# SwiGLU feed-forward on one core: the first loads in line on SyncE, and slice 0 projected ahead of the second transposes

## The chip, the cores and the metric

One Trainium2 chip, one of its cores. A core has a matrix engine (TensorE, "PE"), a vector engine (VectorE, "DVE"), a scalar engine (ScalarE, "ACT"), GpSimd ("POOL") and SyncE ("SP"), each with an instruction queue of its own, and 16 DMA engines that move data between the off-chip memory and the on-chip memory. The metric is the device time of one execution in microseconds (us). The kernel before takes 163.57 us, the median of three runs (163.53 to 163.64).

## The reference

All tensors are bfloat16. The kernel computes a SwiGLU feed-forward block for 2048 rows of 640 columns, with an inner width of 1536:

```python
B, S, D, F = 1, 2048, 640, 1536      # x: [B, S, D]; w_gate, w_up: [D, F]; w_down: [F, D]

def reference(x, w_gate, w_up, w_down):
    g = _silu(x @ w_gate)
    u = x @ w_up
    return (g * u) @ w_down
```

## The kernel before

The rows are worked in four blocks of 512. The gate and up projections are computed transposed: a chunk of 128 inner columns of a weight is the stationary operand, x transposed (`xT`, 128 model columns on the partitions, five such slices of 128) is the moving one, and five matmuls, one for each slice of the model dimension, add up in one bank of PSUM. ScalarE applies Silu to the gate result, VectorE multiplies it with the up result and writes `aT`. When the twelve inner chunks of a block are done, the down projection follows from `aT` and `w_down`. VectorE has a side task: it computes the last four rows of the projections as dot products.

What the change touches is the start, block 0.

Loads. x rows 0-255 are loaded as they lie, in two pieces of 128 rows (line 86, 160 KB each): the first is issued from SyncE, the second from ScalarE. The gate weights of the first four inner chunks (`EARLY`) are loaded as five slices, one for each 128 rows of `w_gate` (line 115, 128 KB each): slice 1 from ScalarE, the others from SyncE. Behind them SyncE issues, in this order, the load that transposes rows 256-511 on the way (`turn_x`, line 105), the up weights of chunks 0-1 and 2-3 (line 83, 320 KB each), the remaining gate and up weights (640 KB each), `w_down` (line 125), and the next block's transposing load. Each DMA has one of eight semaphores in turn; an issue waits until the earlier DMA with its semaphore has landed.

TensorE, in the order in which `head` writes it down (an order that is kept by dependencies without a wait): 18 warm-up matmuls on a tile of ones that nothing reads (line 176); five transposes of x rows 0-127 and five of rows 128-255 (line 185), each group of five in two PSUM tiles, of which ScalarE copies the first (slices 0 and 1) and VectorE the second (slices 2 to 4) to `xT` (line 190); then the gate projection of four chunks at once, in steps of four matmuls (line 193):

```python
steps = [(0, 0, P), (0, P, HALF)]
steps += [(kd, 0, HALF) for kd in range(1, KD)]
steps += [(kd, HALF, S_BLK) for kd in range(KD)]
```

A step is (slice, first column, end column): slice 0 on rows 0-127, on rows 128-255, the slices 1 to 4 on rows 0-255, and all five on rows 256-511, which come by the transposing load. After that the up projection of the four chunks and their gating (lines 214 and 215), and from there the plain loops.

ScalarE issues its two DMAs, loads its table for Silu and runs a dummy Silu (line 119), and then takes its copies.

Of the kernel before, what the change touches and what calls it, by code (L numbers as in the profile page):

```python
# [10 lines left out]
def _body(  # L11
# [8 lines left out]
    nc = tc.nc  # L20
    P = nc.NUM_PARTITIONS
    f32 = mybir.dt.float32
    bf16 = mybir.dt.bfloat16
    ACT = mybir.ActivationFunctionType
# [8 lines left out]
    KD = D // P  # L33
    KF = F // P
    S_BLK = 512
    NSB = S // S_BLK
    SUB = S_BLK // P
    HALF = S_BLK // 2
    DA = 512
    Q = 32  # L40
    N_WARM = 18
    T = 4
    WT_STEP = 4
    ROW_J = 0
    EARLY = 4
# [13 lines left out]
    wg_sb = consts.tile([P, KD, F], bf16)  # L59
# [15 lines left out]
    wg_v = w_gate.rearrange("(kd p) f -> p kd f", p=P)  # L75
# [3 lines left out]
    def wslice(a, b):  # L79
        return slice(a * P, b * P)  # L80
# [4 lines left out]
    def load_x(eng, c0, c1):  # L85
        eng.dma_start(out=x_sb[:, c0:c1, :], in_=x_v[:, c0:c1, :])  # L86
# [11 lines left out]
    def keep_order(engine):  # L98

        traced = [i for i in nc.cur_bb.bb.instructions if i.engine == engine]  # L100
        for a, b in zip(traced, traced[1:]):
            issue_order(a, b)

    def turn_x(r0, r1):
        nc.sync.dma_start_transpose(out=xT[:, :, r0:r1], in_=xt_v[r0:r1])

    ones = consts.tile([P, P], bf16)
    silu_first = consts.tile([P, 1], f32)
    nc.vector.memset(ones[:], 1.0)  # L109

    load_x(nc.sync, 0, 1)
    load_x(nc.scalar, 1, 2)
    for kd in range(KD):
        eng = nc.scalar if kd == 1 else nc.sync
        eng.dma_start(
            out=wg_sb[:, kd, wslice(0, EARLY)], in_=wg_v[:, kd, wslice(0, EARLY)]
        )
    turn_x(HALF, S_BLK)
    nc.scalar.activation(silu_first[:], ones[:, 0:1], ACT.Silu)  # L119
    for a in range(0, EARLY, 2):  # L120
        load_w(nc.sync, wu_sb, wu_v, a, a + 2)
    for a, b in W_CHUNKS:
# [6 lines left out]
    def turn_w(dst, src, f0, f1):  # L129
# [7 lines left out]
        out=x_row[:],  # L137
        in_=x2[S - T : S, :].rearrange("t d -> (t d)").partition_broadcast(P),
# [35 lines left out]
    def warm(n):  # L174
        for _ in range(n):
            nc.tensor.matmul(  # L176
                pw[:, 0:P], lhsT=ones[:], rhs=ones[:], start=True, stop=True
            )

    def transpose_chunk(c, parts):  # L180
        c_sl = slice(c * P, (c + 1) * P)
        for copy, tag, k0, k1 in parts:
            pt = psum.tile([P, k1 - k0, P], bf16, tag=tag, name="pt")
            for kd in range(k0, k1):
                nc.tensor.transpose(  # L185
                    out=pt[:, kd - k0, :],
                    in_=x_sb[:, c, kd * P : (kd + 1) * P],
                    identity=ident[:],
                )
            copy(out=xT[:, k0:k1, c_sl], in_=pt[:])  # L190

    def proj_step(ps, w_sb, fc, sb, c0, c1, kd):
        nc.tensor.matmul(  # L193
            ps[:, c0:c1],
            lhsT=w_sb[:, kd, fc * P : (fc + 1) * P],
            rhs=xT[:, kd, sb * S_BLK + c0 : sb * S_BLK + c1],
            start=(kd == 0 and c0 in (0, HALF)),
            stop=(kd == KD - 1),
        )

    def proj(ps, w_sb, fc, sb, c0, c1):
        for kd in range(KD):
            proj_step(ps, w_sb, fc, sb, c0, c1, kd)
# [6 lines left out]
    def gate(pg, pu, sb, fc, n_s):  # L210

        s0 = sb * S_BLK
        sg = work.tile([P, S_BLK], f32, name="sg")
        nc.scalar.activation(sg[:, 0:n_s], pg[:, 0:n_s], ACT.Silu)  # L214
        nc.vector.tensor_tensor(  # L215
            out=aT[:, fc, s0 : s0 + n_s], in0=sg[:, 0:n_s], in1=pu[:, 0:n_s], op=ALU.mult
        )

    def head():
        dve, act = nc.vector.tensor_copy, nc.scalar.copy  # L220
        split = [(act, "po_a", 0, 2), (dve, "po_b", 2, KD)]
        pgs = [
            psum.tile([P, S_BLK], f32, tag="gu", name="pg", bufs=4)
            for _ in range(EARLY)
        ]
        warm(N_WARM)
        for c in range(HALF // P):
            transpose_chunk(c, split)

        steps = [(0, 0, P), (0, P, HALF)]  # L230
        steps += [(kd, 0, HALF) for kd in range(1, KD)]
        steps += [(kd, HALF, S_BLK) for kd in range(KD)]
        for kd, c0, c1 in steps:
            for fc in range(EARLY):
                proj_step(pgs[fc], wg_sb, fc, 0, c0, c1, kd)

        for fc in range(EARLY):
            pu = psum.tile([P, S_BLK], f32, tag=("po_a", "po_b")[fc % 2], name="pu")
            proj(pu, wu_sb, fc, 0, 0, S_BLK)
            gate(pgs[fc], pu, 0, fc, S_BLK)  # L240
        keep_order(mybir.EngineType.PE)
        keep_order(mybir.EngineType.Activation)

    head()
    for sb in range(NSB):
        n_s = S_BLK if sb < NSB - 1 else S_BLK - T
# [26 lines left out]
        for q in range(P // Q):  # L273
            nc.scalar.dma_start(
                out=out2[
                    sb * S_BLK : sb * S_BLK + n_t, DA + q * Q : DA + (q + 1) * Q
                ].rearrange("(i r) c -> r i c", r=Q),
                in_=ot_q[q * Q : (q + 1) * Q, :].rearrange("r (i c) -> r i c", c=Q),
            )

        for j in range(SUB):
# [6 lines left out]
            for c0, c1, tag in cols:  # L288
# [14 lines left out]
                eng = nc.sync if c1 < D else nc.scalar  # L303
# [82 lines left out]
def kernel(tc, *args):  # L386
    _body(tc, *args)
    tc.close()
    tc.compile()
    _trim(tc.nc)  # L390
# [30 lines left out]
```

## Time and profile before

| | |
|---|---|
| median of three runs | 163.57 us |
| the profiled execution: span from the first to the last instruction (its time as a run is not on the page) | 161.8 us |
| TensorE matmuls, busy | 159.4 us, 99% of the span |
| VectorE, ScalarE busy | 69%, 26% |
| gate projection, all matmuls of line 193 into `pg` | 264, 59.8 us |
| up projection, all matmuls of line 193 into `pu` | 240, 59.1 us |
| warm-up matmuls | 18, 2.1 us |
| HBM read, written | 6.88 MB, 2.62 MB |

The span runs from the first to the last instruction of the profiled execution; the time of a run holds in addition what lies around it. Matmuls are pipelined, so the durations of neighbours overlap; the distance between two starts is what a matmul costs. In a row of the timeline stand the start, the duration, the engine, the line, the operation, what it writes and reads, and in brackets how long the engine stood idle before it and what ended the wait. "PEld" is TensorE's loading of a stationary operand. Lines are those of the kernel before.

### The profile page before, as it was taken

The page shows a single profiled execution, that of the slowest core. Times are in us where ns is not written, and L with a number is a line of the kernel's source. Part 1 is how long each engine was busy: PE and PEld are TensorE (multiplying, and loading weights), DVE is VectorE, ACT ScalarE, POOL GpSimd, SP SyncE. Part 2 cuts the span into 40 slices and gives each one's busy share as a digit, 9 for nine tenths or more (in the row PEclk, how much of TensorE's full clock was granted, in tenths as well). Part 3 has the DMA queues.
Part 4 walks back from the last instruction along what each step waited for, and adds up shares of the span by engine and source line. Part 5 has one row for each costly group of instructions (what it writes and reads, how often), then busy time and mean ns, then how long its engine had stood idle before and what let it go on. Part 6 is the DMA issues. An engine that isn't in the chain of part 4 may idle for free.

```text
span 161.8 us, 2142 instructions
## 1 busy us (share of the span) xinstructions
PE 159.4 (99%) x808; PEld 77.6 (48%) x808; DVE 111.0 (69%) x250; ACT 42.6 (26%) x74; POOL 0.6 (0%) x6
## 2 busy tenths in 40 slices
PE   8999999999999999999999999999999999999995
PEld 7854444444444444444444444444444444445454
DVE  2034223599569999989919999979964999993001
ACT  5051222112222222211222322221214222222121
POOL 1000000000000000000000000000000000000000
PEclk9999999999999999999999999999999999999999
DMA  6999999934189999003110000000321000000312
GB/s 212 231 351 349 361 248 231 222 75 91 34 192 159 235 236 184 4 0 34 65 65 0 0 4 2 0 0 3 62 67 34 0 0 0 0 0 4 48 41 73
DMA packets 41961, 15.86 MB, mean 98 GB/s; under 512 B 33504, under 2 KB 41824, under 8 KB 41952
## 3 DMA queue, kind: packets, MB, share of 16 engines
q1 hardware_dynamic: 33584, 14.93, 37.0%
q10 hardware_dynamic: 8368, 0.80, 3.5%
q8 instruction: 6, 0.10, 0.3%
q14 instruction: 3, 0.02, 0.1%
HBM read 6.88 MB, written 2.62 MB: 59 GB/s over the span
## 4 chain that ended last, share of the span: by engine, by line
PE 97%; DMA 2%; SPq 0%; DVE 0%; issue 0%
PE pg L193 32%; PE pu L193 32%; PE po_a L291 26%; PE po_t L261 6%; DMA wg_sb<-in_w_gate_dram 2%; SPq L86 0%; DVE ot_b L302 0%
## 5 line engine op out<-in xcount | busy, mean ns | idle before, releaser
L193 PE MATMUL pg<-xT,wg_sb 128*128 128x512 bf16 (+3 forms) x264 | 59.8, 363 | 0.1
L193 PE MATMUL pu<-xT,wu_sb 128*128 128x512 bf16 (+1 forms) x240 | 59.1, 379 | 0.0
L215 DVE TENSOR_TENSOR aT<-sg,pu 128x512 bf16<-128x512 f32 (+1 forms) x48 | 32.7, 682 | 32.3 <-PE pu L193 32.3
L214 ACT ACTIVATE sg<-pg 128x512 f32<-128x512 f32 (+1 forms) x48 | 28.4, 597 | 71.2 <-PE pg L193 67.4
L291 PE MATMUL po_a<-wd_sb,aT 128*128 128x512 bf16 (+4 forms) x228 | 42.8, 348 | 0.0
L147 DVE SCALAR_TENSOR_TENSOR prod<-wgT,x_row 128x640 f32<-128x640 bf16 x48 | 39.4, 821 | 1.5 <-DMA wgT<-in_w_gate_dram 0.4
L147 DVE SCALAR_TENSOR_TENSOR prod<-wuT,x_row 128x640 f32<-128x640 bf16 x48 | 39.4, 821 | 1.0
L193 PEld LDWEIGHTS <-wg_sb 128*128 128x128 bf16 x264 | 25.9, 100 | 26.8 <-DMA wg_sb<-in_w_gate_dram 0.4
L193 PEld LDWEIGHTS <-wu_sb 128*128 128x128 bf16 x240 | 23.4, 98 | 28.1 <-DMA wu_sb<-in_w_up_dram 0.3
L291 PEld LDWEIGHTS <-aT 128*128 128x128 bf16 x228 | 20.8, 98 | 21.7
L300 ACT CAST ot<-po_a 128x512 bf16<-128x512 f32 (+2 forms) x17 | 9.5, 559 | 31.8 <-PE po_a L291 20.2
L261 PE MATMUL po_t<-aT,wd_sb 128*128 128x512 bf16 (+1 forms) x48 | 10.4, 366 | 0.0
L261 PEld LDWEIGHTS <-wd_sb 128*128 128x128 bf16 x48 | 4.7, 98 | 5.1
L302 DVE CAST ot_b<-po_a 128x96 bf16<-128x96 f32 (+1 forms) x2 | 0.5, 240 | 9.7 <-PE po_a L291 9.6
L270 ACT CAST ot_t<-po_t 128x512 bf16<-128x512 f32 (+1 forms) x4 | 2.2, 559 | 11.6 <-PE po_t L261 11.6
L147 DVE DVE_READ_ACCUMULATOR prod<-wgT,x_row 128x1 f32 x48 | 3.9, 82 | 0.0
L147 DVE DVE_READ_ACCUMULATOR prod<-wuT,x_row 128x1 f32 x48 | 3.9, 82 | 0.0
L272 DVE STREAM_TRANSPOSE ot_q<-ot_t 128x512 bf16<-128x512 bf16 (+1 forms) x4 | 2.7, 676 | 1.7 <-ACT ot_t L270 1.7
L190 DVE COPY xT<-pt 128x384 bf16<-128x384 bf16 x2 | 0.7, 358 | 2.9 <-PE pt L185 2.9
L176 PE MATMUL pw<-ones 128*128 128x128 bf16 x18 | 2.1, 313 | 0.4 <-DVE ones L109 0.4
L176 PEld LDWEIGHTS <-ones 128*128 128x128 bf16 x18 | 1.8, 147 | 0.4 <-DVE ones L109 0.4
L119 ACT ACT_TABLE_LOAD x1 | 1.3, 1283 | 1.0 <-issue 1.0
(13 smaller groups left out, 4.7 us busy)
## 6 DMA issues: line engine op xcount, KB each, us to landing
wd_sb<-in_w_down_dram SPq DMA_DIRECT2D x1, 1920.0 KB, 13.0
out_dram<-ot SPq DMA_DIRECT2D x15, 128.0 KB, 1.7
wg_sb<-in_w_gate_dram SPq DMA_DIRECT2D x2, 640.0 KB, 7.9
wu_sb<-in_w_up_dram SPq DMA_DIRECT2D x2, 640.0 KB, 8.6
wu_sb<-in_w_up_dram SPq DMA_DIRECT2D x2, 320.0 KB, 4.7
x_row<-in_x_dram SPq DMA_DIRECT2D x1, 640.0 KB, 5.1
wg_sb<-in_w_gate_dram SPq DMA_DIRECT2D x4, 128.0 KB, 3.4
out_dram<-ot_q ACTq DMA_DIRECT2D x12, 32.0 KB, 1.9
```

Of the source, the lines that this page charges most:

```text
L119: nc.scalar.activation(silu_first[:], ones[:, 0:1], ACT.Silu)
L147: nc.vector.scalar_tensor_tensor(out=prod[:], in0=wT[:, fc, :], scalar=1.0, in1=x_row[:, t, :], op0=ALU.mult, op1=ALU.mult, accum_out=acc[ ...
L176: nc.tensor.matmul(pw[:, 0:P], lhsT=ones[:], rhs=ones[:], start=True, stop=True)
L190: copy(out=xT[:, k0:k1, c_sl], in_=pt[:])
L193: nc.tensor.matmul(ps[:, c0:c1], lhsT=w_sb[:, kd, fc * P : (fc + 1) * P], rhs=xT[:, kd, sb * S_BLK + c0 : sb * S_BLK + c1], start=(kd == 0 ...
L214: nc.scalar.activation(sg[:, 0:n_s], pg[:, 0:n_s], ACT.Silu)
L215: nc.vector.tensor_tensor(out=aT[:, fc, s0 : s0 + n_s], in0=sg[:, 0:n_s], in1=pu[:, 0:n_s], op=ALU.mult)
L261: nc.tensor.matmul(po_t[:], lhsT=wd_sb[:, kf, DA:D], rhs=aT[:, kf, sb * S_BLK : sb * S_BLK + n_t], start=(kf == 0), stop=(kf == KF - 1),)
L270: nc.scalar.copy(ot_t[:], po_t[:])
L272: nc.vector.transpose(out=ot_q[:], in_=ot_t[:])
L291: nc.tensor.matmul(po[:], lhsT=aT[:, kf, s0 : s0 + P], rhs=wd_sb[:, kf, c0:c1], start=(kf == 0), stop=(kf == KF - 1),)
L300: nc.scalar.copy(ot[:], po[:])
```

## The change

Loads: SyncE now issues x rows 0-127, slice 0, x rows 128-255, slice 1, and slices 3 and 4 as one DMA of 256 KB, then goes on with the transposing load. ScalarE loads its table and runs the dummy Silu first, and then issues slice 2 as its only load. The DMAs at the start are one fewer, so the first up load gets a semaphore that has not been used, and the numbers of all later ones move by one.

TensorE: 15 warm-ups instead of 18; the transposes of rows 0-127; two more warm-ups; slice 0 on rows 0-127; the transposes of rows 128-255; slice 1 on rows 0-127; slice 0 and slice 1 on rows 128-255; then as before slices 2 to 4 on rows 0-255 and all slices on rows 256-511. Slice 1 is thereby done in 8 matmuls of 128 columns instead of 4 of 256. The lines of the changed kernel move: warm-ups are line 181, transposes 190, copies 195, projection steps 198, the first weight slices 113, x loads 87, the transposing load 106.

```diff
-    N_WARM = 18
+    N_WARM = 15
+    N_GAP = 2
...
+    def load_d(eng, k0, k1):
+        eng.dma_start(
+            out=wg_sb[:, k0:k1, wslice(0, EARLY)], in_=wg_v[:, k0:k1, wslice(0, EARLY)]
+        )
+
+    nc.scalar.activation(silu_first[:], ones[:, 0:1], ACT.Silu)
     load_x(nc.sync, 0, 1)
-    load_x(nc.scalar, 1, 2)
-    for kd in range(KD):
-        eng = nc.scalar if kd == 1 else nc.sync
-        eng.dma_start(
-            out=wg_sb[:, kd, wslice(0, EARLY)], in_=wg_v[:, kd, wslice(0, EARLY)]
-        )
+    load_d(nc.sync, 0, 1)
+    load_x(nc.sync, 1, 2)
+    load_d(nc.sync, 1, 2)
+    load_d(nc.scalar, 2, 3)
+    load_d(nc.sync, 3, KD)
     turn_x(HALF, S_BLK)
-    nc.scalar.activation(silu_first[:], ones[:, 0:1], ACT.Silu)
...
-        warm(N_WARM)
-        for c in range(HALF // P):
-            transpose_chunk(c, split)
-
-        steps = [(0, 0, P), (0, P, HALF)]
-        steps += [(kd, 0, HALF) for kd in range(1, KD)]
-        steps += [(kd, HALF, S_BLK) for kd in range(KD)]
-        for kd, c0, c1 in steps:
+
+        def early_gate(kd, c0, c1):
             for fc in range(EARLY):
                 proj_step(pgs[fc], wg_sb, fc, 0, c0, c1, kd)
+
+        warm(N_WARM)
+        transpose_chunk(0, split)
+        warm(N_GAP)
+        early_gate(0, 0, P)
+        transpose_chunk(1, split)
+        for kd, c0 in ((1, 0), (0, P), (1, P)):
+            early_gate(kd, c0, c0 + P)
+        for kd in range(2, KD):
+            early_gate(kd, 0, HALF)
+        for kd in range(KD):
+            early_gate(kd, HALF, S_BLK)
```

## The prediction

> **What bounds the kernel now.** I read the page first (span, busy shares, chain), then the chain of the first 20 us, the timeline of the first 12 us, and the DMA view by windows, because the change touches only the start.
>
> The page:
>
> ```profile
> span 161.8 us, 2142 instructions
> PE 159.4 (99%) x808; PEld 77.6 (48%) x808; DVE 111.0 (69%) x250; ACT 42.6 (26%) x74; POOL 0.6 (0%) x6
> PE 97%; DMA 2%; SPq 0%; DVE 0%; issue 0%
> ```
>
> TensorE carries the whole program. Only a different start can move the end: every microsecond at which the dense stretch starts earlier or later goes straight into the time. The profiled execution's span is 161.8 us; the median of the runs is 163.57, so 1.8 us lie around the span and the sum is made as a shift of both.
>
> The chain, first 20 us (start, us, what):
>
> ```profile
> 0.45 3.21 DMA wg_sb<-in_w_gate_dram
> 3.66 0.05 issue
> 3.71 5.21 PE pg L193 x44
> 8.92 4.37 PE pu L193 x20
> ```
>
> It blames the slice-0 load (landed 3.66). The timeline shows what it leaves out (start, us, engine, line):
>
> ```profile
> 0.00 0.39 SPq L86 DMA_DIRECT2D x_sb<-in_x_dram  x1
> 0.13 0.38 ACTq L86 DMA_DIRECT2D x_sb<-in_x_dram  x1
> 0.39 2.10 PE L176 MATMUL pw<-ones 128*128 128x128 bf16 x18 [0.39 <-DVE ones L109]
> 0.45 1.84 SPq L115 DMA_DIRECT2D wg_sb<-in_w_gate_dram  x4
> 0.54 0.45 ACTq L115 DMA_DIRECT2D wg_sb<-in_w_gate_dram  x1
> 1.02 1.28 ACT L119 ACT_TABLE_LOAD   x1 [1.02 <-issue]
> 2.31 1.25 PE L185 MATMUL pt<-ident,x_sb 128*128 128x128 bf16 x10
> 2.32 0.20 ACT L119 ACTIVATE silu_first<-ones 128x1 f32<-128x1 bf16 x1
> 2.33 1.91 SPq L105 DMA_TRANSPOSE xT<-in_x_dram  x1
> 2.74 0.37 ACT L190 COPY xT<-pt 128x256 bf16<-128x256 bf16 x1 [0.22 <-PE pt L185]
> 3.06 0.36 DVE L190 COPY xT<-pt 128x384 bf16<-128x384 bf16 x1 [2.73 <-PE pt L185]
> 3.71 4.93 PEld L193 LDWEIGHTS <-wg_sb 128*128 128x128 bf16 x44 [0.41 <-DMA wg_sb<-in_w_gate_dram]
> 4.29 1.15 SPq L83 DMA_DIRECT2D wu_sb<-in_w_up_dram  x2
> ```
>
> And narrower windows of the timeline (a duration runs to the modelled end of its last matmul):
>
> ```profile
> 0.79 1.49 PE L176 MATMUL pw<-ones 128*128 128x128 bf16 x12
> 4.54 0.59 PE L193 MATMUL pg<-xT,wg_sb 128*128 128x256 bf16 x2
> 4.75 0.48 PE L193 MATMUL pg<-xT,wg_sb 128*128 128x256 bf16 x2
> 6.38 0.46 PE L193 MATMUL pg<-xT,wg_sb 128*128 128x256 bf16 x2
> 7.77 1.15 PE L193 MATMUL pg<-xT,wg_sb 128*128 128x256 bf16 x9
> 8.54 0.38 PE L193 MATMUL pg<-xT,wg_sb 128*128 128x256 bf16 x2
> 8.79 0.39 PE L193 MATMUL pu<-xT,wu_sb 128*128 128x512 bf16 x1
> ```
>
> Two things stand there. First, the pace: one warm-up lasts about 0.31 us, so 12 of them start (1.49 - 0.31) / 11 = 0.107 us apart; nine 256-column matmuls at 7.77 start (1.15 - 0.27) / 8 = 0.110 apart, half the time per column. The rows at 4.54 and 4.75 are still 0.21 apart, the next ones 0.11: the clock step lies at 4.95. Second, two waits that the chain hides: at 6.38 the next matmul follows only after 0.46 - 0.27 = 0.19 us, so 0.08 are lost; at 8.54 the two leave TensorE free at 8.54 + 0.11 + 0.11 = 8.76, and the first up-projection starts at 8.79. Both wait for loads (KB each, us from issue to landing; the DMA view by windows that hold one issue each, and its DMA row for the first 20 us):
>
> ```profile
> x_sb<-in_x_dram SPq DMA_DIRECT2D x1, 160.0 KB, 2.3
> x_sb<-in_x_dram ACTq DMA_DIRECT2D x1, 160.0 KB, 2.6
> wg_sb<-in_w_gate_dram SPq DMA_DIRECT2D x1, 128.0 KB, 3.2
> wg_sb<-in_w_gate_dram ACTq DMA_DIRECT2D x1, 128.0 KB, 3.3
> wg_sb<-in_w_gate_dram SPq DMA_DIRECT2D x1, 128.0 KB, 3.4
> xT<-in_x_dram SPq DMA_TRANSPOSE x1, 4.2
> wu_sb<-in_w_up_dram SPq DMA_DIRECT2D x1, 320.0 KB, 4.5
> DMA  0079998889993699999999999999999999999999
> ```
>
> The transposed rows 256-511 land at 2.33 + 4.2 = 6.53, the first up weights at 4.29 + 4.5 = 8.79. The DMA row (busy tenths in half-microsecond slices of the first 20 us) stands at 8 or 9 from 1.5 us on, but for a dip at 6.0 to 7.0 around the end of the transposing load. So TensorE, although it seems to be the bound, is twice held by a stream of loads in line. Work that it gets done sooner before 6.5 us is worth nothing unless that stream moves too.
>
> **The change part by part.**
>
> *Loads.* The bytes are the same: 2 x 160 KB of x, 5 x 128 KB of gate slices, 960 KB ahead of the transposing load. From x 0-127 (2.3) to the last slice (issued as the fourth on SP at about 1.85, + 3.4 = 5.25) 800 KB land in 2.95 us: 271 KB/us. In the new order on SyncE I estimate by that rate: slice 0 at 2.3 + 0.47 = 2.77, x 128-255 at 3.36, slice 1 at 3.83, the rest by 5.25. For slice 0 the other end is its landing now, 3.66. I take the lower one, since only 160 KB instead of up to 448 KB then stand ahead of or beside it.
> The Trainium skill, "DMA: Bandwidth & Descriptors", section "Issuing engines are not separate DMA queues", says that DMAs of all engines share the same 16 DMA engines and that several issuers save only issue time. By it the 960 KB are done at the same 5.25, and lining up on SP can lose issue time but not win bytes; the DMA row, nearly full throughout, agrees.
>
> *x 0-127* no longer shares its first half microsecond with x 128-255. It lands between 1.7 us after its issue, which a lone 128 KB store takes, and the present 2.3:
>
> ```profile
> out_dram<-ot SPq DMA_DIRECT2D x15, 128.0 KB, 1.7
> ```
>
> But 15 warm-ups end at 0.39 + 15 x 0.107 = 1.99, so the first transpose starts between 1.99 and 2.31. I take 2.15, the middle, because x 128-255 comes only 0.13 later now and shares a part of it, not all.
>
> *TensorE's order*, from 2.15: five transposes x 0.107 to 2.68; two fillers to 2.90. ScalarE's copy came 2.74 - 2.31 = 0.43 after the first transpose and took 0.37, so slice 0 can start at 2.15 + 0.80 + 0.04 = 3.0: four matmuls to 3.43. Second transposes (x there at 3.36) to 3.96; slice 1 on rows 0-127 to 4.39; slice 0 on rows 128-255 (copy done at 3.43 + 0.80 = 4.23) to 4.82; slice 1 there, over the clock step, to 5.10; slices 2 to 4, 12 x 0.109, to 6.41. With a first transpose at 2.31 or 1.99 it is 6.51 or 6.33. Now TensorE is ready at 6.49 (6.38 + 0.11) and goes on at 6.57. The fillers (2 x 0.107) stand inside the wait for the copy and cost nothing; the four extra matmuls and weight loads (slice 1 in two halves) cost nothing while cold, since 2 x 0.107 is the 0.21 of one of 256 columns. Three warm-ups fewer leave up to 0.32 us idle if x lands as now.
>
> *ScalarE.* The table load and the dummy Silu (1.28 + 0.20) go ahead of its one DMA, slice 2: issued at about 0.13 + 1.48 + 0.05 = 1.66 instead of slice 1 at 0.54. With the 3.3 us of that row it lands at 4.96 and is needed at 5.10: covered by 0.14; without that, the excess is the cost. ScalarE is free for its first copy either way.
>
> *SyncE.* Five issues still stand ahead of the transposing load; the last fetches two slices. It takes between 0.46 (1.84 / 4) and 0.58 (1.15 / 2, five times the rows of one slice). Hence that load is issued at 2.33 to 2.45; I take 2.36, near the row it resembles. It landed 4.2 after issue behind the slices; a 512-row one on an idle queue shows the floor:
>
> ```profile
> 44.58 2.73 SPq L105 DMA_TRANSPOSE xT<-in_x_dram  x1
> xT<-in_x_dram SPq DMA_TRANSPOSE x1, 5.4
> ```
>
> Less half of its 2.73 us of issue that is 4.0 for 256 rows. Landing: 2.33 + 4.0 = 6.33 to 2.45 + 4.2 = 6.65; I take 6.50, nearer to the present order since the bytes ahead are the same. The up weights, which are queued behind it and lose a wait that had long been met, follow at the same distance: 8.76. The loads behind them keep order and distance.
>
> *Sum.* TensorE ready at 6.41, rows landed 6.50, resumed at 6.54 against 6.57; 20 x 0.109 later 8.72, up weights 8.76 against 8.79. The gain is 0.03, with the roundings 0 to 0.1: 163.5. About 0.2%, 0.33 us, is what a measurement of this kernel tells from no change.
>
> **The rivals.**
> *Slice 0 stays late.* If it lands at 3.66 as now, it blocks the second transposes, which stand behind it in TensorE's queue. Slice 0 ends at 4.14, the transposes at 4.67, slice 1 on rows 0-127 about 5.0, then 8 x 0.055 and 12 x 0.109: 6.75, 0.18 later than 6.57: 163.75, still within 0.2%. For it speaks that 3.66 is a measured row; against it that less stands ahead.
>
> *The stream drains sooner.* x at 1.99, the transposing load at its floor (6.33): TensorE ready at 6.33, resumed at 6.37, 0.2 less: 163.35. Over 0.33 needs the clock step earlier as well: with it 0.3 us earlier TensorE is ready 0.15 sooner and the rows must land by 6.2, which only a start of its packets ahead of the last slices gives: 163.1.
>
> *The clock step comes later.* This one ends slower. Each microsecond that it lies behind 4.95 costs 1 - 0.0545 / 0.107 = 0.49 us, less the 0.07 between ready and landed. It decides from (0.33 + 0.07) / 0.49 = 0.8 us on; a step two microseconds later gives 0.9: 164.5. For it speaks that the step follows from TensorE's business, and the new order moves idle time from 3.3-3.7 to 2.0-2.3 and 2.9-3.0; against it that the idle total, about 0.4, stays.
> The three runs (163.53 to 163.64) leave room for only about 0.2 us of jitter in the step.
> The Trainium skill, "TensorE: Matmul & The Clock Gate", section "What's actually happening", has a free-running window of 3413 ns and a transition varying by 500 ns; by that, a step 0.5 us off would be 0.25 us of time, and a missed window 1.7. The spread of the runs does not bear out such a jitter.
>
> **How the numbers follow.** The forecast holds with 0.45 and the late slice 0 with 0.12: both within 0.2%, 0.57. The sooner stream beyond 0.2% gets 0.20; the later step, or a stall of that size elsewhere in the start, 0.23. The range goes to 163.1 (stream and step sooner) and 164.2 (a step 1.4 us late).
>
> **What would show it.** Right: first transpose between 2.0 and 2.3, slice 0's matmuls near 3.0 with the second transposes behind them, no 0.41 wait for the slice ahead of them, the step at 4.95, and still a wait for the transposed rows near 6.5 and for the up weights near 8.75. Wrong: slice 0 starting past 3.4, 256-column matmuls 0.21 apart after 5.2, or the transposing load landing outside 6.3 to 6.65.

## The result and the profile after

The changed kernel takes 165.51 us, the median of six runs (164.17 to 165.77), against 163.60 (163.53 to 163.99) for the kernel before. The ratio is 1.0097, 95% interval 1.007 to 1.0124: slower by 1%, where I had forecast 163.5 and no change. The profiled execution of the changed kernel took 165.74 and has a span of 164.4 us; before it was 161.8. The runs that list both have a time 1.3 us above their span (163.64 with 162.3), so the profiled execution before was one of about 163.1, an estimate, and faster than its median: of the 2.6 us between the spans, the medians show 1.9.

Several kernels below have runs in two groups 1.5 to 2 us apart; medians are over all runs, while the intervals leave out runs more than 1.5% above the fastest of a kernel, so that for a kernel with two groups the ratio lies below what its median says.

The page of the changed kernel:

```profile
span 164.4 us, 2135 instructions
...
PE 160.2 (97%) x799; PEld 78.3 (48%) x811; DVE 111.1 (68%) x250; ACT 42.6 (26%) x74; POOL 0.6 (0%) x6
...
PE 95%; DMA 3%; SPq 1%; issue 1%; DVE 0%
```

The span grew by 2.6 us, TensorE's busy time by only 0.8: TensorE stands idle longer. Where, the chain of the first 20 us says (start, us, what):

```profile
0.91 0.43 SPq L87
1.34 0.04 issue
1.39 4.17 DMA wg_sb<-in_w_gate_dram
5.55 0.05 issue
5.60 5.98 PE pg L198 x44
```

The load that starts the dense stretch is no longer slice 0 but slice 1, the fourth piece in SyncE's line: issued at 1.39, landed at 5.55. The timeline of the first 12 us:

```profile
0.12 1.28 ACT L117 ACT_TABLE_LOAD   x1
...
0.38 0.42 ACTq L113 DMA_DIRECT2D wg_sb<-in_w_gate_dram  x1
...
0.40 1.78 PE L181 MATMUL pw<-ones 128*128 128x128 bf16 x15 [0.40 <-DVE ones L110]
...
2.32 0.71 PE L190 MATMUL pt<-ident,x_sb 128*128 128x128 bf16 x5
...
2.34 1.53 SPq L106 DMA_TRANSPOSE xT<-in_x_dram  x1
...
3.33 0.61 PE L198 MATMUL pg<-xT,wg_sb 128*128 128x128 bf16 x4
...
3.74 0.73 PE L190 MATMUL pt<-ident,x_sb 128*128 128x128 bf16 x5
...
5.60 5.98 PE L198 MATMUL pg<-xT,wg_sb 128*128 128x128 bf16 x44 [1.13 <-DMA wg_sb<-in_w_gate_dram]
```

TensorE is idle from 2.0 to 2.32 (x as late as before), 0.28 us ahead of slice 0, and from 4.27 (3.74 + 5 x 0.107) to 5.60 ahead of slice 1. Two narrower windows show what that did to its pace:

```profile
8.13 1.05 PE L198 MATMUL pg<-xT,wg_sb 128*128 128x256 bf16 x4
...
9.24 2.02 PE L198 MATMUL pg<-xT,wg_sb 128*128 128x256 bf16 x17
```

At 8.13 matmuls of 256 columns start (1.05 - 0.41) / 3 = 0.21 apart, from 9.24 on (2.02 - 0.27) / 16 = 0.109: the clock step that stood at 4.95 before stands at 9.0. The loads, from the DMA view by windows in the order of issue (x 0-127, slice 2, slice 0, x 128-255, slice 1, slices 3-4, transposed rows), and the DMA row of the first 20 us:

```profile
x_sb<-in_x_dram SPq DMA_DIRECT2D x1, 160.0 KB, 2.3
...
wg_sb<-in_w_gate_dram ACTq DMA_DIRECT2D x1, 128.0 KB, 2.6
...
wg_sb<-in_w_gate_dram SPq DMA_DIRECT2D x1, 128.0 KB, 2.8
...
x_sb<-in_x_dram SPq DMA_DIRECT2D x1, 160.0 KB, 2.8
...
wg_sb<-in_w_gate_dram SPq DMA_DIRECT2D x1, 128.0 KB, 4.2
...
wg_sb<-in_w_gate_dram SPq DMA_DIRECT2D x1, 256.0 KB, 4.4
...
xT<-in_x_dram SPq DMA_TRANSPOSE x1, 5.2
...
DMA  0078998688959999999999999999999999999999
GB/s 0 0 136 270 328 333 203 121 231 264 230 94 242 310 231 289 291 293 301 344 344 354 340 354 348 340 358 340 350 352 356 336 342 360 361 353 353 369 366 366
```

Between 3.0 and 4.0 us (the seventh and eighth slice) the stream falls to 203 and 121 GB/s, with slices 1, 3 and 4 issued and not landed. In the kernel before the same slices hold 262 and 258:

```profile
GB/s 0 0 179 360 303 326 262 258 283 210 243 232 79 183 280 326 331 349 347 367 346 334 367 363 352 352 344 377 336 336 346 348 350 361 362 366 361 366 358 361
```

This hole, as it is called below, is no idle stretch of the DMA engines: the DMA row counts the engines as busy 0.8 and 0.6 of these two slices. The trace shows why both can be: 7 of the 169 packets (the single transfers that a DMA is made of) that start between 3.0 and 4.0 last 0.32 to 1.07 us, where a packet of a gate slice usually takes 0.046; before, 2 of 284 are that long.

The same 960 KB that were in by 5.25 are in at 1.86 + 4.4 = 6.25, and the transposed rows come at 2.34 + 5.2 = 7.54 instead of 6.53.

From these rows the profiled execution's 2.6 us can be divided, as an estimate: from 5.60 the rest of the first half at full pace, 12 x 0.055 + 12 x 0.109 = 1.97, would end at 7.57, just as the transposed rows land; TensorE would go on at about 7.6 instead of 6.57. That is 1.0 us of late loads. The remaining 1.6 is the clock step, which made those 24 matmuls end near 9.2.

### The profile page after: what moved, and what is told of

Same layout as the page of the kernel before. It is cut to its first block, busy times and chain, and to the rows that moved or that the text cites. A ratio compares the mean times of both kernels' runs of the same rounds, so it can differ in the third digit from the quotient of the medians.

```text
span 164.4 us, 2135 instructions
## 1 busy us (share of the span) xinstructions
PE 160.2 (97%) x799; PEld 78.3 (48%) x811; DVE 111.1 (68%) x250; ACT 42.6 (26%) x74; POOL 0.6 (0%) x6
## 4 chain that ended last, share of the span: by engine, by line
PE 95%; DMA 3%; SPq 1%; issue 1%; DVE 0%
PE pg L198 32%; PE pu L198 31%; PE po_a L302 26%; PE po_t L272 6%; DMA wg_sb<-in_w_gate_dram 3%; SPq L87 1%; SPq L113 0%; DVE ot_b L313 0%
## 5 line engine op out<-in xcount | busy, mean ns | idle before, releaser
L198 PE MATMUL pg<-xT,wg_sb 128*128 128x512 bf16 (+3 forms) x262 | 60.8, 367 | 1.5 <-DMA wg_sb<-in_w_gate_dram 1.1
L198 PEld LDWEIGHTS <-wg_sb 128*128 128x128 bf16 x268 | 26.7, 103 | 28.4 <-DMA wg_sb<-in_w_gate_dram 1.7
L190 PE MATMUL pt<-ident,x_sb 128*128 128x128 bf16 x10 | 1.4, 310 | 0.1
```

The costliest lines, as they stand in the source:

```text
L190: nc.tensor.transpose(out=pt[:, kd - k0, :], in_=x_sb[:, c, kd * P : (kd + 1) * P], identity=ident[:],)
L198: nc.tensor.matmul(ps[:, c0:c1], lhsT=w_sb[:, kd, fc * P : (fc + 1) * P], rhs=xT[:, kd, sb * S_BLK + c0 : sb * S_BLK + c1], start=(kd == 0 ...
```

## The experiments

**The loads alone, and TensorE's order alone.**

```diff
 e1_loads, against the kernel before
-    load_x(nc.scalar, 1, 2)
...
+    nc.scalar.activation(silu_first[:], ones[:, 0:1], ACT.Silu)
     load_x(nc.sync, 0, 1)
+    load_d(nc.sync, 0, 1)
+    load_x(nc.sync, 1, 2)
+    load_d(nc.sync, 1, 2)
+    load_d(nc.scalar, 2, 3)
+    load_d(nc.sync, 3, KD)
     turn_x(HALF, S_BLK)
...
 e2_order, against the kernel before
-    N_WARM = 18
+    N_WARM = 15
+    N_GAP = 2
...
+        warm(N_WARM)
+        transpose_chunk(0, split)
+        warm(N_GAP)
+        early_gate(0, 0, P)
+        transpose_chunk(1, split)
+        for kd, c0 in ((1, 0), (0, P), (1, P)):
+            early_gate(kd, c0, c0 + P)
...
```

> The new order of the loads alone; TensorE keeps its old order and its 18 warm-ups. Theory (loads): the line on SyncE brings x 128-255 at about 3.7 and slice 1 at about 5.5 instead of 2.7 and 3.9, TensorE then stands idle for over 1 us before 5.5 and the clock step moves behind it: 164.5 to 165.8, as the whole change. Rival (TensorE's order): the loads cost little by themselves and the time stays at 163.4 to 163.9.

> TensorE's new order alone (15 warm-ups, 2 fillers, slice 0 on rows 0-127 ahead of the second transposes, slice 1 in halves); the loads as before. Theory (loads): slice 0 lands near 3.7 and holds the second transposes back, TensorE loses at most 0.2 us and the step stays near 5: 163.4 to 163.9. Rival (TensorE's order): the idle time moved ahead of the step puts it off: 164.3 or more.

The loads alone give 165.25 us against 163.71, ratio 1.0093 (1.0061 to 1.0124): the whole loss. Slice 1 lands at 5.43 and the step comes at 9.0, as in the changed kernel; here TensorE's long wait is for x rows 128-255, 0.9 us ahead of the second transposes. TensorE's order alone gives 163.83, ratio 1.0014 (0.999 to 1.0038): no difference. In the profile of the latter slice 0 landed at 3.18 and was not late at all; one of its 12 runs took 165.41.

**Fillers where TensorE waits for slice 1.**

```diff
 e3_fill, against the changed kernel
         transpose_chunk(1, split)
+        pf = psum.tile([P, S_BLK], f32, tag="po_a", name="pf")
+        for _ in range(12):
+            nc.tensor.matmul(pf[:, 0:P], lhsT=ones[:], rhs=ones[:], start=True, stop=True)
```

> The changed kernel with 12 filler matmuls on the tile of ones right behind the second transposes, where TensorE stood idle from 4.5 to 5.6 in the changed kernel. Theory (the loss is partly the clock): the step comes at 5 to 5.6 instead of 9.0; with slice 1 still late, 12 half-width steps and 12 of 0.109 end near 7.6, the second half near 9.8 instead of 11.4: about 164.0, 1.5 less than the changed kernel. Rival (the loss is the late loads alone): the fillers change nothing, 165.5.

Median 164.29 (1.0066, 1.0034 to 1.0098). Eight of the 12 runs lie between 163.57 and 164.60, four between 165.59 and 165.81. The profiled run, one of the first group, has slice 1 at 5.20, yet the fillers already run at full pace (chain of the first 20 us; 12 of them in 0.68 us, 0.057 each):

```profile
4.53 0.68 PE pf L243 x12
5.21 0.04 issue
5.25 4.38 PE pg L198 x44
```

So 12 matmuls that compute nothing take 1.2 us off the median of the changed kernel. The four late runs have no profile; that the step is missed there is inferred from their distance, 1.7 us between the medians of the two groups. Nor does the profile show the fillers bringing the step: it came at 4.43, with the first of them, after 0.7 us of idle time. Up to its long gap the changed kernel had been idle for about as long (0.63), so it is that gap which sets it apart.

**Every idle stretch filled.**

```diff
 e10_fillall, against e3_fill
-    N_WARM = 15
-    N_GAP = 2
+    N_WARM = 18
+    N_GAP = 5
...
-        for _ in range(12):
+        for _ in range(14):
```

> The changed kernel with every idle stretch of TensorE ahead of slice 1 filled: 18 warm-ups, 5 fillers ahead of slice 0, 14 behind the second transposes. The loads stay late. Theory (two parts: the step, about 1.2 us, and the transposed rows landing 0.6 to 1.0 later): the step comes near 5 in all runs, no run over 165, median 164.0 to 164.5. Rival (fillers catch the step in some runs only): a second group at 165.5 and above, as with 12 fillers.

Median 164.31, ratio 1.0038 (1.0022 to 1.0054); ten of 11 runs lie between 163.72 and 164.68, one at 166.64, so "no run over 165" holds for all but one. What is left against the kernel before is 0.7 us of the median. I expected the late transposed rows to be its cause, but the profile shows another: x rows 128-255 land only at 4.32, slice 1 is in at 4.96, and the fillers hold TensorE until 6.17:

```profile
4.36 0.71 PE L190 MATMUL pt<-ident,x_sb 128*128 128x128 bf16 x5 [0.34 <-DMA x_sb<-in_x_dram]
4.87 1.46 PE L243 MATMUL pf<-ones 128*128 128x128 bf16 x14
6.17 4.33 PE L198 MATMUL pg<-xT,wg_sb 128*128 128x128 bf16 x44
```

TensorE is ready for the transposed rows at 6.17 + 1.97 = 8.14, 0.8 after they landed at 7.37. So in this run the fillers themselves held it up, and how the 0.7 divides between loads and fillers is open. The missed step is worth at least 165.51 - 164.31 = 1.2 us of the median, as far as two kernels measured on different occasions can tell; the two groups of runs of e3_fill, e8_swap and e11_xback lie 1.6 to 1.8 apart.

**Idle time alone.** The loads and the order of the kernel before, 14 warm-ups fewer:

```diff
 e6_warm4, against the kernel before
-    N_WARM = 18
+    N_WARM = 4
```

> The kernel before with 4 warm-ups instead of 18, so that TensorE is idle from about 0.9 to 2.3; its loads and its order are untouched. Theory (idle time ahead of the step puts the step off): the loads land as before, the step moves from about 5 to 7 or more in most runs: median 164.3 to 165.5. Rival (the step keeps its time, only late loads cost): 163.5 to 163.9.

164.12 us, ratio 1.0032 (1.0018 to 1.0047): slower, though by less than expected. The profiled run is one of the slowest (164.61) and shows the mechanism bare: 1.52 us of idle time ahead of the first transposes (1.7 by the distance of the starts, which is how idle time is counted in the last section), no wait for a load after that, matmuls (1.06 - 0.42) / 3 = 0.21 apart still at 7.41, and 0.11 from 8.43:

```profile
2.53 1.25 PE L185 MATMUL pt<-ident,x_sb 128*128 128x128 bf16 x10 [1.52 <-DMA x_sb<-in_x_dram]
...
7.41 1.06 PE L193 MATMUL pg<-xT,wg_sb 128*128 128x256 bf16 x4
...
8.43 1.04 PE L193 MATMUL pg<-xT,wg_sb 128*128 128x256 bf16 x8
```

So idle time alone puts the step off, with the loads and the order untouched. Where the step lay in the eleven other runs, up to 0.8 us faster than this one, no profile shows.

**What makes slice 1 late.** Four kernels test that.

```diff
 e4_split, against the changed kernel: no merged load
-    load_d(nc.sync, 3, KD)
+    load_d(nc.sync, 3, 4)
+    load_d(nc.sync, 4, KD)
...
 e5_turnlate, against the changed kernel: the transposing load goes behind the first two up loads
-    turn_x(HALF, S_BLK)
     for a in range(0, EARLY, 2):
         load_w(nc.sync, wu_sb, wu_v, a, a + 2)
+    turn_x(HALF, S_BLK)
...
 e9_places, against the changed kernel: third and fourth place exchanged
-    load_x(nc.sync, 1, 2)
     load_d(nc.sync, 1, 2)
+    load_x(nc.sync, 1, 2)
...
 e11_xback, against the changed kernel: x 128-255 on ScalarE, ahead of slice 2
-    load_x(nc.sync, 1, 2)
+    load_x(nc.scalar, 1, 2)
```

> The changed kernel with slices 3 and 4 as two DMAs again. Theory (the line of loads is the cause, not the merging): slice 1 lands past 5 all the same, 165 to 165.8, or up to 0.5 worse, since a sixth issue puts the transposing load off by 0.45 us. Rival (the DMA of two slices, twice the rows in one issue, holds up the slice ahead of it): slice 1 lands by 4.5 and the time is 164.0 or less.

> The changed kernel with the transposing load of rows 256-511 issued behind the first two up loads. Read from the trace, not from the time. Theory (its issue, 1.5 to 1.9 us of SyncE's, makes the pause in SyncE's stream between 3.3 and 4.2): slice 1 lands by 4.3 and no pause stands there. Rival (the pause comes from the line of small loads itself): slice 1 lands past 4.8 all the same. In both the transposed rows land about 2 us later, so the time is 165 to 167.

> The changed kernel with slice 1 ahead of x 128-255 in SyncE's line: the same DMAs, two places exchanged. Theory (the fourth place lands at 4.8 to 5.5, whatever it holds, and the third near 3.7): slice 1 lands near 3.7, x 128-255 near 5; TensorE then waits for x instead, as long as before: 165.0 to 165.8. Rival (slice 1 itself is slow to fetch): slice 1 past 4.8 in the third place, too.

> The changed kernel with x 128-255 back on ScalarE, ahead of slice 2; SyncE's line has x 0-127, slice 0, slice 1, slices 3-4. Theory (what hurts is five pieces in line on one queue, with slice 1 in the fourth place): slice 1 lands by 4.5, the transposed rows by 6.9, 163.5 to 164.0. Rival (the merged slices or the early table load are at fault): 165 or more.

With the merged load split again the time is 165.32 (1.0109, 1.008 to 1.0138) and slice 1 lands at 5.04: the merging is not the cause. With the transposing load later (one run, 165.66) its issue begins at 3.44 instead of 2.34, and the hole of the DMA row stands where it stood, 178 and 88 GB/s between 3.0 and 4.0, slice 1 at 1.38 + 3.6 = 4.99:

```profile
GB/s 0 0 136 292 336 306 178 88 313 350 347 346 322 284 220 211 298 283 369 371 359 375 342 358 348 342 356 338 352 383 322 346 361 360 363 360 358 366 358 366
```

So the transposing load's issue is not the cause either. With the places exchanged (166.33, ratio 1.0152, 1.0127 to 1.0176, worse than expected) slice 1 lands at 0.91 + 3.4 = 4.3, not near 3.7, and x 128-255 at 1.39 + 3.8 = 5.15, issue and landing of each in this order:

```profile
wg_sb<-in_w_gate_dram SPq DMA_DIRECT2D x1, 128.0 KB, 3.4
...
x_sb<-in_x_dram SPq DMA_DIRECT2D x1, 160.0 KB, 3.8
```

The place is late, not the tensor. With x 128-255 back on ScalarE, and the early table load kept, the hole is gone (299 and 352 GB/s between 3.0 and 4.0), and the transposed rows land at 6.38, earlier than in the kernel before:

```profile
GB/s 0 0 164 287 252 352 299 352 334 224 290 205 254 258 321 336 323 345 348 344 350 348 348 350 342 352 375 332 340 350 358 347 358 368 358 361 364 364 364 366
```

Its time missed my expectation, however: five runs lie between 163.08 and 164.13, seven between 165.13 and 166.06, median 165.21 (the ratio, over the seven fastest runs, is 1.0033, 1.0003 to 1.0063). The loads are mended; the idle stretches are not. The profiled run (163.08) caught the step at 3.9 in spite of three waits:

```profile
2.37 0.72 PE L190 MATMUL pt<-ident,x_sb 128*128 128x128 bf16 x5 [0.20 <-DMA x_sb<-in_x_dram]
...
3.47 0.57 PE L198 MATMUL pg<-xT,wg_sb 128*128 128x128 bf16 x4 [0.17 <-DMA wg_sb<-in_w_gate_dram]
...
4.56 4.34 PE L198 MATMUL pg<-xT,wg_sb 128*128 128x128 bf16 x44 [0.23 <-DMA wg_sb<-in_w_gate_dram]
```

I have no profile of a run of the second group; that those missed the step is inferred from the size of the difference.

**Which slice stands in the late place.**

```diff
 e8_swap, against the changed kernel
-    load_d(nc.sync, 1, 2)
-    load_d(nc.scalar, 2, 3)
+    load_d(nc.scalar, 1, 2)
+    load_d(nc.sync, 2, 3)
```

> The changed kernel with slice 1 on ScalarE and slice 2 in its place in SyncE's line. Theory (the fourth place in the line falls into the pause, and slice 1 was the first one needed): slice 1 lands near 3.0, slice 2 near 5.4, just when TensorE comes to it; the gap of 1.1 us is gone and the step comes near 5 in most runs; the transposed rows still land near 7.4, 0.9 later than before: 164.2 to 164.7. Rival (the transposed rows and the step are late all the same): 165.2 or more.

Median 164.15 (1.0039, 1.0019 to 1.0059): eight runs between 163.78 and 164.20, four between 165.18 and 166.25. The profiled run is one of the four, and the hole there hit even the third place, x 128-255, which landed at 4.70; the step came at 9.9. The median is 0.05 below the range of the theory, and the profile shows a run in which the theory fails: the wait for slice 1 is gone, but one of 0.93 us for x 128-255 stands ahead of it.

**Two attempts at something faster.** TensorE's new order with the old loads and 18 warm-ups, and the kernel before with fillers in its own wait for slice 0:

```diff
 e7_order18, against e2_order
-    N_WARM = 15
+    N_WARM = 18
...
 e12_before3, against the kernel before
+        pf = psum.tile([P, S_BLK], f32, tag="po_a", name="pf")
+        for _ in range(3):
+            nc.tensor.matmul(pf[:, 0:P], lhsT=ones[:], rhs=ones[:], start=True, stop=True)
         for kd, c0, c1 in steps:
```

> TensorE's new order with the loads of before, and 18 warm-ups instead of 15, so that no idle time stands ahead of the first transposes. Theory (what jitter there was came from the missing warm-ups): 163.3 to 163.8, no run over 164.5, step near 5. Rival (the order itself costs): 163.9 or more.

> The kernel before with 3 filler matmuls in the 0.41 us in which it waits for slice 0. Theory (the spread of its runs is the jitter of the step, and idle time ahead of it makes it worse): median 0.1 to 0.3 below the kernel before, spread smaller. Rival (0.41 of idle time doesn't matter to the step): same median within 0.1.

163.49 against 163.65, ratio 0.9997 (0.9983 to 1.0011), all runs at or below 164.36; and 163.77 against 163.60, ratio 1.0012 (0.9998 to 1.0026). Neither differs from the kernel before, so the missing three warm-ups explain no measurable part. The second says little on filling: in its profile slice 0 had landed at 3.41, before the fillers began at 3.66, so there was no wait left to fill. No kernel tried beats the kernel before.

## Why the prediction was wrong

*The loads.* This is the step that failed. I let the pieces land in the order of their issue at the mean rate of 271 KB/us: slice 1 at 3.83, the rest by 5.25. Measured: 5.55 and 6.25. Two things are in that. Slice 2, 128 KB, was issued early and landed ahead of slice 0 (see ScalarE below). With it the same rate gives 3.24 for slice 0, 3.83 for x 128-255 and 4.30 for slice 1; the first two came at 3.28 and 3.69, so the rate held up to there. Slice 1 came 1.25 later still, and that is the hole, which a mean rate can't show.

My own quoted rows had another rule: the fourth SyncE issue before, at 1.38, landed after 3.4 us, at 4.8. By its place alone slice 1 would have been given 4.8, 0.8 after my 3.96 for the end of the second transposes, and that would have been a warning. But this rule isn't right here either: the second and third place came 0.4 and 0.8 sooner than before (3.28 against 3.66, 3.69 against 4.50), the fourth 0.7 later and the fifth 1.0 later. What I asked of slice 0, whether it keeps the landing of its place, I did not ask of slice 1, which moved from ScalarE's second to SyncE's fourth.

The Trainium skill, "DMA: Bandwidth & Descriptors", section "Issuing engines are not separate DMA queues", from which I took that the bytes are done at the same time however they are issued, does not hold in these runs. With x 128-255 issued from ScalarE in place of SyncE as the only edit (e11_xback) the 960 KB were in at 1.39 + 3.8 = 5.2 instead of 6.25, while the saved issue is 0.47.

*x 0-127* was forecast at 2.15, measured at 2.27: no sooner than before, so the shorter warm-up left 0.35 us idle. *Slice 0* came at 3.28, between my two ends (that only 160 KB stood ahead of or beside it was wrong, slice 2 came too); TensorE took it at 3.33 instead of 3.0, the second transposes at 3.74 instead of 3.43. Small, and within the bounds.

*ScalarE.* I had slice 2 issued at 1.66, behind the table load and the dummy Silu. It was issued at 0.38, while the table load ran from 0.12 to 1.41. The DMA did not wait for it. Thus slice 2, which is needed late, landed first of all slices, at 2.99, and shared the DMA engines with slice 0.

*SyncE and the transposed rows.* The issue at 2.34 was right (2.36), the landing wrong: 7.54 against 6.33 to 6.65, since the pieces ahead of it were late. The first up weights landed at 8.72, as forecast (8.76), but by luck: they were to follow the transposed rows at the distance of before, and came 1.2 behind them instead of 2.26. Nothing waited for them, since TensorE reached them only after 11.3.

*The clock step.* I had it as the rival that ends slower, with 0.23, its price of 0.49 per microsecond and a point of 0.8 us from which it decides. The mechanism and the price were right: between the two profiles it moved 4 us, and the idle time ahead of slice 1 puts it off, as the fillers show over the runs and e6_warm4 shows for idle time alone. What failed is the argument against it, that the idle total stays at 0.4: it is 2.0 us in the profile after, because the loads are late. I also read three runs as a bound on the jitter of the step. The kernel before, run 28 times beside the last experiments, spreads from 163.16 to 164.17, and the step in the profiles of kernels with under 0.9 us of idle time lies between 3.9 and 5.9. The Trainium skill's page "TensorE: Matmul & The Clock Gate", which has a free-running window of 3413 ns in the section "What's actually happening", is borne out there, against what I concluded: the traces show its length (last section), and the estimate of 1.7 us for a missed window that I set aside is what lies between the groups, 1.6 to 1.8. The spread of 2 us is wider than the 500 ns to either side that the section gives.

*The span.* That 1.8 us lie around it was a misreading, as said above: it is 1.3. The sum does not rest on it.

*The rest.* That the fillers and the split of slice 1 cost nothing holds (the order alone, 1.0014). That there is next to nothing to win at the start is not contradicted: with the transposed rows at 6.38 (x 128-255 back on ScalarE) the fastest run took 163.08, against 163.16 for the fastest of the kernel before beside it.

What stays open is the hole itself: why packets take so long between 3.2 and 4.0 us and the stream falls. Between 3.5 and 4.0 it stands at 67 to 121 GB/s in all eight profiles with one load on ScalarE and 832 KB of x and gate slices on SyncE, and at no less than 201 in the six with two loads on ScalarE and 672 KB on SyncE. The number of pieces in SyncE's line isn't it: the kernel before has five there, too. Excluded are the merged load, the transposing load's issue, the early table load and the tensor in the place; the bytes in the line and the number of loads on ScalarE were not varied apart.

## What to carry to other kernels

When a load is moved to another queue or another place in a line, take both its landing by the mean rate and that of its place in the trace, let the later one be the bound, and ask of each piece who waits for it; here even the later one, 4.8, was 0.7 short. In the first microseconds idle time of TensorE costs twice: the wait itself and, if it is long enough, a missed clock step, 1.2 us of the median here and 1.6 to 1.8 for a run that misses it. Fillers on a constant tile help against that; they are free only while they end before the load lands (e3_fill), and not when they run on behind it (e10_fillall). Two or three runs don't show the jitter of the step; a kernel that is near it falls into two groups.

## What the runs showed of the hardware that I had not expected

Over the profiled start, as far as one profile for each kernel tells, more idle time goes with more late runs: with 0.3 to 0.45 us of it ahead of the step (the kernel before, e7_order18, e12_before3) no run was over 164.5; with 0.6 (e2_order, e10_fillall) one of 12 and one of 11 were over 165; with 0.7 to 0.8 (e3_fill, e11_xback) four and seven of 12; with 1.3 to 2.1 (e1_loads, e4_split, e9_places, the changed kernel) 20 of 24 (of e8_swap, with 1.7, one of the four late runs was profiled; e5_turnlate has one run). The 1.7 us of e6_warm4, which end at 2.5, cost less: no run of 12 over 164.62, though the step of the profiled one came at 8.4.

What decides, the 14 traces say together, is not the total but the idle time within one window of 3.41 us. Four of them hold records of the granted clock. The record of the full clock begins at 4.95 (the kernel before), 5.84 (e2_order), 4.12 (e7_order18) and 5.92 (e12_before3), within 0.04 of the step as the spacing of the matmuls shows it, and lasts 157.013 us in three and 160.426 in one: 46 and 47 times 3.413. Taking windows of that length back from the step, the one that ends at the step holds at most 0.78 us of idle time in all 14 profiles (0.78 in e11_xback, 0.70 in e3_fill, 0.36 before). In the seven with a step after 8 us the window ahead of that one holds at least 0.92 (0.92 in e6_warm4, 1.03 in e4_split, 1.76 in the changed kernel). So in these runs a window with 0.92 us or more of idle time did not bring the step, and it came at the end of the next one. By that, an estimate, the step of e6_warm4 lies between 5.0 and 8.4, since a window that ends after 5.02 holds less than 0.92 us of its idle time; the profiled run, with 8.43, is then near its worst. This was read from the traces afterwards; no experiment was made to test it.

ScalarE's sequencer issued a DMA during a table load that stands ahead of it in its queue (0.38 against 0.12 to 1.41).

The granted clock is listed as 1.0 for the whole span of every run, the half-paced stretch included, and ten of the 14 traces hold no record of it at all; the pace has to be read from the distance between matmuls.
